# Bucketed attention with a feed-forward block on one core: keys-first scores in place of row-normalised, transposed weights

## The chip, the cores and the metric

The kernel runs on 1 core of one Trainium2 chip. The number that counts is the time of one execution on the chip in microseconds (us). Three runs of the kernel before gave 1418.2, 1417.16 and 1420.69 us; their median is 1418.2 us.

## The reference

`q`, `k` and `v` have shape (4 batches, 8 heads, 768 tokens, 64 channels). Each query and each key gets a bucket number from six hash bits, the signs of its products with the six columns of `proj`. A query attends only to the keys of its own bucket.

```
q_bits = (einsum('bhsd,dk->bhsk', q, proj) > 0);  k_bits likewise
mask   = bucket(q)[..., :, None] == bucket(k)[..., None, :]
scores = where(mask, q @ k.T / sqrt(64), -1e9)
attn   = exp(scores - max(scores));  attn /= sum(attn) + 1e-9
x      = (attn @ v), heads side by side: 3072 tokens x 512 channels
h      = x @ w_in            # 512 x 2048
out    = (h * sigmoid(1.702 h)) @ w_out   # 2048 x 512
```

The inputs `q`, `k` and `v` are normal numbers times 0.1. The weights arrive as float64 and are turned into float32 on the chip.

## The kernel before

**Attention.** Work goes by 16 pairs of heads (4 batches by 4 pairs). A pair's two heads lie side by side on the 128 partitions, 64 channels each. `prepare` turns the keys and queries so that channels lie on partitions (12 TensorE transposes, L143, evicted by VectorE at L146 and by ScalarE at L149), and makes the hash bits with one matmul per half of the tokens (L151) and a VectorE comparison (L152).

The 768 queries of a pair are two halves of three tiles of 128. `scores` takes one tile of queries by all 768 keys: for each head and each half of the keys a bfloat16 matmul on the hash bits and a float32 matmul on the channels add into one PSUM tile (L167). Each float32 matmul stands in the trace as two MATMUL records. VectorE then evicts each head's 128x768 scores with the mask's clamp and the row minimum (L173; scores are kept negated), ScalarE takes the exponential with that minimum as its bias and the row sum (L175), VectorE makes the reciprocals (L177, L178), and GpSimd multiplies the rows by them (L180). `turn` transposes the finished weights, six 128x128 transposes per head (L190), so that keys lie on partitions; VectorE and ScalarE evict them (L195, L193). `values` multiplies them with `v` (L203), 12 matmuls per half, and ScalarE evicts the result into `xT` (L206).

**Weights.** `convert` turns one 128x256 piece of a float64 weight into float32: a load on GpSimd's queue (L87), five VectorE operations (L94 to L99), two GpSimd operations (L102, L103), and one more on VectorE (L104). There are 64 pieces.

**Feed-forward block.** Then 384 matmuls 128x512 give `h` (L249), ScalarE applies the activation (L251), 384 more give `y` (L255), VectorE evicts (L258), and the SP queue stores (L260).

**Order of the work.** A scheduler places each engine's instructions, TensorE's too, by its own estimates of when they are ready. Each engine then takes its instructions strictly in that order. `turn` and `values` of a tile are emitted behind the scores of the next one. PSUM holds two buffers of four kinds of tile: `ps` (scores), `pt` (transposed weights), and `m` for hash, turned inputs and `av`.

Of the kernel before, what the change touches and what calls it, by code (L numbers as in the profile page):

```python
# [9 lines left out]
BF16 = mybir.dt.bfloat16  # L10
U32 = mybir.dt.uint32
Act = mybir.ActivationFunctionType
Alu = mybir.AluOpType
PSUM = bass.MemoryType.PSUM

P = 128
# [3 lines left out]
BIT = 2.0**33  # L20


@with_exitstack
def kernel(
# [26 lines left out]
    assert D == 64 and S == 2 * HS and HS <= 512 and HP == KC and DM <= 512 and NB < 32  # L51
# [3 lines left out]
    make_identity(nc, ident)  # L55

    # The hash of two heads at once: head j's channels give its bits on rows 64 j to 64 j + NB.
# [5 lines left out]
    # Bits become +-0.5 (0 on rows without one). Row NB is a constant: with it, the product of a  # L63
    # query's and a key's column is 0 where all bits agree, and -0.5 for each bit that differs.
# [13 lines left out]
    w_out_sb = const.tile([P, FC, DM], F32, name="w_out_sb")  # L78

# [1 line left out]
    actx = ExitStack()  # L81
    cv = actx.enter_context(tc.tile_pool(name="cv", bufs=2))
    CW = 256

    def convert(dst, src):
        raw = cv.tile([P, CW, 2], U32, tag="raw", name="raw")
# [5 lines left out]
        rest = cv.tile([P, CW], F32, tag="rest", name="rest")  # L92
        # Sign, exponent (rebiased by its top bit) and the upper 20 bits of the mantissa.
# [3 lines left out]
        # The mantissa's lower 32 bits, scaled by the power of two that is `bits` without mantissa.  # L97
        nc.vector.tensor_scalar(sign, bits, 0xFF800000, None, op0=Alu.bitwise_and)
        nc.vector.scalar_tensor_tensor(rest, lo, 2.0**-52, sign.bitcast(F32), op0=Alu.mult, op1=Alu.mult)  # L99
# [3 lines left out]
        nc.gpsimd.tensor_tensor(rest, bits.bitcast(F32), rest, op=Alu.add)  # L103
        nc.vector.scalar_tensor_tensor(dst, size, (1.125 * 2.0**-15) ** 2, rest, op0=Alu.is_ge, op1=Alu.mult)  # L104
# [7 lines left out]
    ld = actx.enter_context(tc.tile_pool(name="ld", bufs=2))  # L112
    wk = actx.enter_context(tc.tile_pool(name="wk", bufs=2))
    sp = actx.enter_context(tc.tile_pool(name="sp", bufs=5))
    pp = actx.enter_context(tc.tile_pool(name="pp", bufs=4))
    st = actx.enter_context(tc.tile_pool(name="st", bufs=4))
    sps = actx.enter_context(tc.tile_pool(name="sps", bufs=2, space=PSUM))
    tps = actx.enter_context(tc.tile_pool(name="tps", bufs=2, space=PSUM))
    mps = actx.enter_context(tc.tile_pool(name="mps", bufs=2, space=PSUM))

    pairs = [(b, hp) for b in range(B) for hp in range(HP)]
    loaded, ready = {}, {}

    def load(n):
        b, hp = pairs[n]
        for name, src in (("k", k), ("q", q), ("v", v)):
            # Both heads' channels of a token side by side, so that one transpose turns them.
            x = ld.tile([P, T, 2, D], F32, tag=name, name=name, bufs=2 if name == "v" else 1)
            for j in range(2):
                nc.sync.dma_start(out=x[:, :, j, :], in_=src[b, 2 * hp + j].rearrange("(p t) d -> p t d", p=P))  # L130
            loaded[n, name] = x

    def prepare(n):
        """The pair's queries and keys, channels first, and their hash bits."""
        for name, off, op in (("k", k_off, Alu.is_gt), ("q", q_off, Alu.is_lt)):
            x = loaded.pop((n, name))
            xt = wk.tile([P, S], F32, tag=f"{name}T", name=f"{name}T")
            bits = wk.tile([P, S], BF16, tag=f"{name}b", name=f"{name}b")
            for c in range(2):
# [5 lines left out]
                if name == "k":  # L145
                    nc.vector.tensor_copy(xt[:, cols], tp)  # L146
                else:
                    # Negated and scaled by a power of two, for the scores; its bits read "below 0".
                    nc.scalar.mul(xt[:, cols], tp, -1.0 / D**0.5)  # L149
# [3 lines left out]
            if name == "q":  # L153
                nc.vector.tensor_scalar(bits, bits, -BIT, None, op0=Alu.mult)
            ready[n, name] = xt, bits

    def scores(n, t):
        """exp(score - its row's max) / (sum + 1e-9) of both heads, queries of tile t by all keys."""
        (qT, qb), (kT, kb) = ready[n, "q"], ready[n, "k"]
        rows = slice(t * P, (t + 1) * P)  # L160
        ps = [sps.tile([P, 2, 512], F32, tag="s", name="ps") for _ in range(2)]
        for c in range(2):
            cols = slice(c * HS, (c + 1) * HS)
            for a, m, last in ((qb, kb, False), (qT, kT, True)):
                for j in range(2):
                    hs = slice(D * j, D * (j + 1))
                    nc.tensor.matmul(ps[j][:, c, 0:HS], a[hs, rows], m[hs, cols], start=not last, stop=last)  # L167
        low = st.tile([P, 2], F32, tag="low", name="low")
        total = st.tile([P, 2], F32, tag="total", name="total")
        es = []  # L170
        for j in range(2):
            e = sp.tile([P, 2, HS], F32, tag="e", name="e")
# [3 lines left out]
            es.append(e.rearrange("p c s -> p (c s)"))  # L176
        nc.vector.tensor_scalar_add(total, total, 1e-9)  # L177
        nc.vector.reciprocal(total, total)  # L178
        for j in range(2):
            nc.gpsimd.tensor_scalar(es[j], es[j], total[:, j : j + 1], 1.0, op0=Alu.mult, op1=Alu.mult)  # L180
        return es
# [25 lines left out]

    load(0)
    prepare(0)
    behind = []  # L210

    def catch_up():
        for f, *a in behind:
# [74 lines left out]
```

## Time and profile before

| what | value |
|---|---|
| median of the runs | 1418.2 us |
| profiled execution, its span | 1420.0 us |
| TensorE busy (PE) | 1314.6 us, 93% of the span |
| VectorE busy (DVE) | 513.9 us, 36% |
| ScalarE busy (ACT) | 358.9 us, 25% |
| GpSimd busy (POOL) | 300.1 us, 21% |
| mean granted TensorE clock | 0.970 of full |
| first matmul of the feed-forward block | at 756.50 us |

Busy shares are means over stages. Three stages can be told apart: attention with the weight conversion beside it (to some 345 us), attention alone (to 756 us), and the feed-forward block. The profile gives the span of one execution from the first to the last instruction; it lies 0.13% above the median of the runs, so times of the trace can be set against the runs directly.

### The profile page before, as it was taken

The page shows a single profiled execution, that of the slowest core. Times are in us where ns is not written, and L with a number is a line of the kernel's source. Part 1 is how long each engine was busy: PE and PEld are TensorE (multiplying, and loading weights), DVE is VectorE, ACT ScalarE, POOL GpSimd, SP SyncE. Part 2 cuts the span into 40 slices and gives each one's busy share as a digit, 9 for nine tenths or more (in the row PEclk, how much of TensorE's full clock was granted, in tenths as well). Part 3 has the DMA queues.
Part 4 walks back from the last instruction along what each step waited for, and adds up shares of the span by engine and source line. Part 5 has one row for each costly group of instructions (what it writes and reads, how often), then busy time and mean ns, then how long its engine had stood idle before and what let it go on. Part 6 is the DMA issues. An engine that isn't in the chain of part 4 may idle for free.

```text
span 1420.0 us, 13204 instructions
## 1 busy us (share of the span) xinstructions
PE 1314.6 (93%) x4928; PEld 657.7 (46%) x4928; DVE 513.9 (36%) x1299; ACT 358.9 (25%) x738; POOL 300.1 (21%) x390
## 2 busy tenths in 40 slices
PE   5887887888999999999989999999999999999998
PEld 3443443444555555555554444444444444444443
DVE  6788888887555555555540000000000000000000
ACT  1333333334444444444442100100100100100100
POOL 4555555554222232222230000000000000000000
PEclk9898898899999999999999999999999999999999
DMA  5132222221111111111000000000000000000000
GB/s 130 56 79 71 67 78 71 67 78 49 31 26 34 34 34 23 23 33 24 12 1 0 0 15 15 0 15 15 0 15 15 0 15 15 0 8 22 0 8 22
DMA packets 84062, 42.79 MB, mean 30 GB/s; under 512 B 76832, under 2 KB 76832, under 8 KB 84000
## 3 DMA queue, kind: packets, MB, share of 16 engines
q1 hardware_dynamic: 78880, 25.18, 7.1%
q0 software_dynamic: 5120, 16.78, 3.8%
q8 instruction: 39, 0.64, 0.2%
q14 instruction: 23, 0.19, 0.0%
HBM read 35.65 MB, written 6.29 MB: 30 GB/s over the span
## 4 chain that ended last, share of the span: by engine, by line
PE 75%; DVE 12%; POOL 4%; ACT 4%; DMA 2%; issue 2%; POOLq 0%; DVEq 0%; ACTq 0%
PE h L249 23%; PE y L255 23%; PE ps L167 12%; PE av L203 7%; PE pt L190 7%; ACT e L175 3%; DVE e L173 3%; POOL e L180 2%; PE hash L151 2%; DMA raw<-in_moe_w_in_dram 2%; POOL rest L103 2%; DVE pT L195 2%; DVE sign L94 1%; DVE rest L99 1%; DVE bits L95 1%
## 5 line engine op out<-in xcount | busy, mean ns | idle before, releaser
L249 PE MATMUL h<-xT,w_in_sb 128*128 128x512 f32 x768 | 330.7, 592 | 0.6 <-ACT xT L206 0.6
L255 PE MATMUL y<-w_out_sb,g 128*128 128x512 f32 x768 | 330.6, 592 | 0.0
L258 DVE COPY o<-y 128x512 f32<-128x512 f32 x24 | 16.6, 690 | 648.8 <-PE y L255 648.8
L180 POOL TENSOR_SCALAR e<-e,total 128x768 f32<-128x768 f32 x192 | 177.3, 934 | 322.8 <-ACT pT L193 212.9
L167 PE MATMUL ps<-kT,qT 64*128 64x384 f32 x768 | 241.8, 527 | 0.0
L175 ACT ACTIVATE e<-e,low 128x768 f32<-128x768 f32 x192 | 179.4, 934 | 210.0 <-DVE e L173 208.0
L249 PEld LDWEIGHTS h<-xT,w_in_sb 128*128 128x128 f32 x768 | 145.8, 190 | 184.4 <-issue 183.2
L255 PEld LDWEIGHTS y<-w_out_sb,g 128*128 128x128 f32 x768 | 145.9, 190 | 183.7 <-issue 183.7
L173 DVE TENSOR_SCALAR_CACHE_REDUCE e<-ps 128x768 f32<-128x768 f32 x192 | 176.6, 953 | 139.0 <-PE ps L167 139.0
L190 PE MATMUL pt<-ident,e 128*128 128x128 f32 x1152 | 180.2, 295 | 33.7 <-POOL e L180 32.4
L190 PEld LDWEIGHTS pt<-ident,e 128*128 128x128 f32 x1152 | 133.9, 149 | 139.6 <-issue 63.1
L251 ACT ACTIVATE g<-h 128x512 f32<-128x512 f32 x96 | 57.3, 597 | 542.7 <-PE h L249 542.7
L167 PE MATMUL ps<-kb,qb 64*128 64x384 bf16 x384 | 99.6, 347 | 53.0 <-DVE e L173 52.8
L167 PEld LDWEIGHTS ps<-kT,qT 64*128 64x128 f32 x768 | 107.8, 203 | 83.0 <-issue 82.9
L203 PE MATMUL av<-pT,v 128*64 128x384 f32 x768 | 145.6, 499 | 0.0
L195 DVE COPY pT<-pt 128x384 f32<-128x384 f32 x192 | 106.0, 552 | 21.2 <-PE pt L190 20.5
L193 ACT COPY pT<-pt 128x384 f32<-128x384 f32 x192 | 89.9, 468 | 64.1 <-PE pt L190 62.9
L203 PEld LDWEIGHTS av<-pT,v 128*64 128x64 f32 x768 | 73.1, 139 | 57.9 <-issue 31.8
L103 POOL TENSOR_TENSOR rest<-bits,rest 128x256 f32<-128x256 f32 x64 | 47.6, 743 | 61.6 <-DVE rest L99 42.0
L102 POOL TENSOR_TENSOR size<-raw 128x256 f32<-128x256 f32 x64 | 41.4, 647 | 63.6 <-DMA raw<-in_moe_w_in_dram 29.1
L206 ACT COPY xT<-av 128x384 f32<-128x384 f32 x32 | 15.3, 478 | 128.1 <-PE av L203 128.1
L167 PEld LDWEIGHTS <-qb 64*128 64x128 bf16 x384 | 24.2, 94 | 44.7 <-issue 41.9
(41 smaller groups left out, 517.5 us busy)
## 6 DMA issues: line engine op xcount, KB each, us to landing
raw<-in_moe_w_in_dram POOLq DMA_DIRECT2D x32, 256.0 KB, 3.1
raw<-in_moe_w_out_dram POOLq DMA_DIRECT2D x32, 256.0 KB, 3.1
k<-in_k_dram SPq DMA_DIRECT2D x32, 192.0 KB, 3.2
q<-in_q_dram SPq DMA_DIRECT2D x32, 192.0 KB, 3.2
v<-in_v_dram SPq DMA_DIRECT2D x32, 192.0 KB, 3.4
out_dram<-o SPq DMA_DIRECT2D x24, 256.0 KB, 2.0
pb<-in_proj_dram SPq DMA_DIRECT2D x2, 1.5 KB, 3.0
```

Source lines behind the costliest of these rows:

```text
L103: nc.gpsimd.tensor_tensor(rest, bits.bitcast(F32), rest, op=Alu.add)
L167: nc.tensor.matmul(ps[j][:, c, 0:HS], a[hs, rows], m[hs, cols], start=not last, stop=last)
L173: nc.vector.tensor_scalar(e, ps[j][:, :, 0:HS], MASKED, None, op0=Alu.min, op1=Alu.min, accum_out=low[:, j : j + 1])
L175: nc.scalar.activation(e, e, Act.Exp, bias=low[:, j : j + 1], scale=-1.0, accum_out=total[:, j : j + 1])
L180: nc.gpsimd.tensor_scalar(es[j], es[j], total[:, j : j + 1], 1.0, op0=Alu.mult, op1=Alu.mult)
L190: nc.tensor.transpose(tp[:, i, :], es[j][:, s : s + P], ident)
L193: nc.scalar.copy(dst, tp)
L195: nc.vector.tensor_copy(dst, tp)
L203: nc.tensor.matmul(av[D * j : D * (j + 1), :], vt[:, t, j, :], pT[j][:, t, :], start=(t == 0), stop=(t == T - 1))
L249: nc.tensor.matmul(h, w_in_sb[:, kc, fc * P : (fc + 1) * P], xT[:, kc, n * NT : (n + 1) * NT], start=(kc == 0), stop=(kc == KC - 1))
L251: nc.scalar.activation(g[:, fc, :], h, Act.Gelu_apprx_sigmoid)
L255: nc.tensor.matmul(y, g[:, fc, i * P : (i + 1) * P], w_out_sb[:, fc, :], start=(fc == 0), stop=(fc == FC - 1))
```

## The change

The scores are computed with keys on partitions and queries along the free axis, one tile of 128 keys by one half (384) of the queries, both heads in one PSUM tile. ScalarE takes the exponential straight out of PSUM, without a row maximum, into a buffer `es` of the half. This buffer is already what the product with `v` needs, so the transposes, the normalising multiplication and the clamp are gone. A half now has six such units. The sums over keys are built by VectorE and GpSimd adding the six exponential tiles (`sums`), and a matmul with a tile of ones adds over the partitions (`norm`); a reciprocal and one VectorE operation write `xT`. A 385th column of the exponentials holds a tiny constant.

Leaving out the maximum is safe only for small scores. ScalarE therefore sums the squares of each pair's queries and keys (`measure`). After the feed-forward block every engine loads the largest of them and branches: if it is at least 64, attention in the old way and the feed-forward block run again.

TensorE's instructions in attention now keep the order in which the code emits them (`manual_schedule`); the other engines are scheduled as before. The weight pieces are 128x512, so there are 32 of them, and three of their working tiles have one buffer in place of two.

```diff
-    CW = 256
+    CW = 512
-            nc.vector.tensor_scalar(e, ps[j][:, :, 0:HS], MASKED, None, op0=Alu.min, op1=Alu.min,
-                                    accum_out=low[:, j : j + 1])
-            nc.scalar.activation(e, e, Act.Exp, bias=low[:, j : j + 1], scale=-1.0, accum_out=total[:, j : j + 1])
-        nc.vector.tensor_scalar_add(total, total, 1e-9)
-        nc.vector.reciprocal(total, total)
-        for j in range(2):
-            nc.gpsimd.tensor_scalar(es[j], es[j], total[:, j : j + 1], 1.0, op0=Alu.mult, op1=Alu.mult)
-    def turn(es, t, pT):
...
+            es = [ep.tile([P, T, 2, HS + 1], F32, name=f"e{i}") for i in range(2)]
...
+            def measure(n):
+                for i, name in enumerate("kq"):
...
+                    nc.scalar.activation(junk, tiles[n][name], Act.Square,
+                                         accum_out=sizes[:, 2 * n + i : 2 * n + i + 1])
+            def scores(n, c, kt):
...
+                ps = sps.tile([P, 2, 512], F32, tag="s", name="ps")
+                for a, m, last in ((kb, qb, False), (kT, qT, True)):
+                    for j in range(2):
+                        hs = slice(D * j, D * (j + 1))
+                        nc.tensor.matmul(ps[:, j, 0:HS], a[hs, keys], m[hs, cols], start=not last, stop=last)
+                nc.scalar.activation(es[c][:, kt, :, 0:HS], ps[:, :, 0:HS], Act.Exp)
+            def sums(n, c, kt):
...
+                if kt == 1:
...
+                    nc.vector.scalar_tensor_tensor(acc, e[:, 0, :, 0:HS], T * TINY, e[:, 1, :, 0:HS],
+                                                   op0=Alu.add, op1=Alu.add)
+                elif kt == 3:
...
+                    nc.gpsimd.tensor_tensor(two, e[:, 2, :, 0:HS], e[:, 3, :, 0:HS], op=Alu.add)
+                elif kt > 3:
...
+                    nc.vector.tensor_tensor(acc, acc, e[:, kt, :, 0:HS], op=Alu.add)
+                    if kt == T - 1:
+                        nc.vector.tensor_tensor(acc, acc, accs.pop((n, c, 2)), op=Alu.add)
+            def values(n, c, kt):
...
+                for j in range(2):
+                    nc.tensor.matmul(av[D * j : D * (j + 1), :], vt[:, kt, j, :], es[c][:, kt, j, :],
+                                     start=(kt == 0), stop=(kt == T - 1))
+            def norm(n, c):
...
+                for j in range(2):
+                    nc.tensor.matmul(dn[D * j : D * (j + 1), :], ones, acc[:, j, :], start=True, stop=True)
+                rd = st.tile([P, HS], F32, tag="rd", name="rd")
+                nc.vector.reciprocal(rd, dn)
...
+                nc.vector.scalar_tensor_tensor(xT[:, hp, s0 : s0 + HS], av[:, 0:HS], vs[:, 0:1], rd,
+                                               op0=Alu.add, op1=Alu.mult)
+            with tc.manual_schedule(engines={PE}):
...
+                LAG = 2
...
+                    for u in range(2 * T):
+                        c, kt = divmod(u, T)
+                        scores(n, c, kt)
+                        behind.append((n, c, kt))
+                        sums(n, c, kt)
+                        if len(behind) > LAG:
+                            x = behind.pop(0)
+                            values(*x)
+                            if x[2] == T - 1:
+                                norm(x[0], x[1])
+                        if u >= 1 and todo:
+                            todo.pop(0)()
...
+    attention()
+    feed_forward("")
+    unsafe = nc.values_load(largest[0:1, 0:1].bitcast(I32)) >= SAFE_BITS
+    with tc.If(unsafe):
+        shifted_attention()
+        feed_forward("2")
```

On TensorE, in the first pairs of heads before: score matmuls of the two heads (`ps`) lie apart, with transposed weights (`pt`), hash and turned queries (`tp`) between them.

```order
L167 LDWEIGHTS qb
L167 MATMUL ps<-kb,qb 128x384
L167 LDWEIGHTS qb
L167 MATMUL ps<-kb,qb 128x384
L190 MATMUL pt<-ident,e 128x128 x6
L167 MATMUL ps<-kT,qT 128x384
L151 MATMUL hash<-qT,pb 128x384
L143 MATMUL tp<-ident,q 128x128 x3
L167 MATMUL ps<-kT,qT 128x384
L151 MATMUL hash<-qT,pb 128x384
```

On TensorE now, in the middle of attention (the tenth of 16 pairs, where the next pair's queries are hashed): four score matmuls stand together, then the two products with `v` of two units earlier, then one step of the next pair's preparation.

```order
L210 MATMUL ps<-qT,kT 128x384 x2
L237 MATMUL av<-e_111,v 64x385 x2
L165 MATMUL hash<-qT,pb 128x384
L210 LDWEIGHTS kb
L210 MATMUL ps<-qb,kb 128x384
L210 LDWEIGHTS kb
L210 MATMUL ps<-qb,kb 128x384
L210 MATMUL ps<-qT,kT 128x384 x2
L237 MATMUL av<-e_111,v 64x385 x2
L165 MATMUL hash<-qT,pb 128x384
```

The two heads' matmuls of one kind now follow each other throughout, and no transposes of weights are left.

On VectorE before, while weights are converted (`raw`, `bits`, `sign`, `rest` are the conversion's tiles): between the conversion's operations stand score evictions out of PSUM (`e`) and evictions of transposed weights (`pT`).

```order
L195 COPY pT<-pt 128x3x128 [waits PE_49]
L178 RECIPROCAL total<-total 128x2 [waits DVE_49]
L104 SCALAR_TENSOR_TENSOR w_in_sb<-size,rest 128x256 [waits Pool_49]
L96 TENSOR_TENSOR bits<-bits,sign 128x256
L173 TENSOR_SCALAR e,low<-ps 128x768 [waits PE_49] x2
L195 COPY pT<-pt 128x3x128 [waits PE_49]
L146 COPY kT<-tp 128x384 [waits PE_49]
L98 TENSOR_SCALAR sign<-bits 128x256 [waits DVE_49]
L94 TENSOR_SCALAR sign<-raw 128x256 [waits DMASW1_49]
L99 SCALAR_TENSOR_TENSOR rest<-raw,sign 128x256 [waits DVE_49]
```

On VectorE now, in the same stage (from the second pair to the third; `acc` and `two` are the running sums):

```order
L228 TENSOR_TENSOR acc<-acc,e_111 128x768 [waits Activation_49]
L120 SCALAR_TENSOR_TENSOR w_in_sb<-size,w_in_sb 128x512 [waits Pool_49]
L230 TENSOR_TENSOR acc<-acc,two 128x768 [waits DVE_49]
L111 TENSOR_SCALAR bits<-raw 128x512
L112 TENSOR_TENSOR bits<-bits,sign 128x512 [waits DVE_49]
L114 TENSOR_SCALAR sign<-bits 128x512 [waits DVE_49]
L115 SCALAR_TENSOR_TENSOR w_in_sb<-raw,sign 128x512 [waits DVE_49]
L220 SCALAR_TENSOR_TENSOR acc<-e_110 128x768 [waits Activation_49]
L247 RECIPROCAL rd<-dn 128x384 [waits PE_49]
L249 COPY vs<-av 128x1
L158 COPY kT<-tp 128x384 [waits PE_49]
L251 SCALAR_TENSOR_TENSOR xT<-av,vs,rd 128x384 [waits DVE_49]
```

Most of VectorE's work between conversions now reads SBUF. All 32 conversions stand ahead of the twelfth of the 32 `xT` operations (L251) in this queue, nearly three to a half; from there on the queue holds none.

## Rows read from the trace of the kernel before

**Rows 1.** Busy time by stretch: stretch, its length, PE, PEld, DVE, ACT, POOL, granted clock, DMA.

```profile
core 0: us, PE busy (x) PEld busy (x) DVE busy (x) ACT busy (x) POOL busy (x), PEclk, DMA share, GB/s
54.63:341.20 286.57, 229.91 (x1158) 124.33 (x1157) 241.43 (x621) 101.90 (x219) 164.99 (x227) 0.88 0.25 71
364.40:756.50 392.10, 367.07 (x1994) 211.38 (x1993) 200.44 (x507) 175.38 (x375) 101.64 (x114) 0.99 0.10 23
```

**Rows 2.** Groups by line in those two stretches, ACT: count, busy us, mean ns.

```profile
L206 ACT COPY xT<-av 128x384 f32<-128x384 f32 x11 | 5.3, 479 | 44.7 <-PE av L203 44.7
...
L206 ACT COPY xT<-av 128x384 f32<-128x384 f32 x20 | 9.6, 478 | 79.1 <-PE av L203 79.1
```

**Rows 3.** Timeline of PE near 510 us: start, us, what, count, [idle before].

```profile
504.89 0.33 PE L167 MATMUL ps<-kb,qb 64*128 64x384 bf16 x1
...
506.38 0.87 PE L190 MATMUL pt<-ident,e 128*128 128x128 f32 x6
507.18 4.52 PE L203 MATMUL av<-pT,v 128*64 128x384 f32 x24
511.64 0.34 PE L167 MATMUL ps<-kb,qb 64*128 64x384 bf16 x2
511.81 0.81 PE L167 MATMUL ps<-kT,qT 64*128 64x384 f32 x4
512.55 0.87 PE L190 MATMUL pt<-ident,e 128*128 128x128 f32 x6
...
518.66 0.49 PE L143 MATMUL tp<-ident,k 128*128 128x128 f32 x3
519.08 0.33 PE L167 MATMUL ps<-kb,qb 64*128 64x384 bf16 x1
...
520.70 0.81 PE L151 MATMUL hash<-kT,pb 128*128 128x384 f32 x2
521.35 0.49 PE L143 MATMUL tp<-ident,k 128*128 128x128 f32 x3
```

**Rows 4.** Groups by line of the whole span, shapes apart.

```profile
L190 PE MATMUL pt<-ident,e 128*128 128x128 f32 x1152 | 180.2, 295 | 33.7 <-POOL e L180 32.4 <-ACT pT L193 1.2
L175 ACT ACTIVATE e<-e,low 128x768 f32<-128x768 f32 x192 | 179.4, 934 | 210.0 <-DVE e L173 208.0 <-POOL e L180 1.9
L103 POOL TENSOR_TENSOR rest<-bits,rest 128x256 f32<-128x256 f32 x64 | 47.6, 743 | 61.6 <-DVE rest L99 42.0 <-DVE total L177 17.6 <-DVE total L178 2.0
L102 POOL TENSOR_TENSOR size<-raw 128x256 f32<-128x256 f32 x64 | 41.4, 647 | 63.6 <-DMA raw<-in_moe_w_in_dram 29.1 <-DMA raw<-in_moe_w_out_dram 22.6 <-DVE pT L195 2.7
L177 DVE TENSOR_SCALAR total<-total 128x2 f32<-128x2 f32 x96 | 15.8, 164 | 42.4 <-ACT e L175 42.4
L178 DVE RECIPROCAL total<-total 128x2 f32<-128x2 f32 x96 | 15.0, 156 | 0.8 <-DVE sign L94 0.2
```

**Rows 5.** Timeline of DVE near 176 us, GpSimd idle beside it.

```profile
175.59 0.55 DVE L195 COPY pT<-pt 128x384 f32<-128x384 f32 x1
176.06 0.28 DVE L98 TENSOR_SCALAR sign<-bits 128x256 uint32<-128x256 uint32 x1
176.26 0.29 DVE L94 TENSOR_SCALAR sign<-raw 128x256 uint32<-128x256 uint32 x1
176.46 0.42 DVE L99 SCALAR_TENSOR_TENSOR rest<-raw,sign 128x256 f32<-128x256 uint32 x1
176.79 0.29 DVE L95 TENSOR_SCALAR bits<-raw 128x256 uint32<-128x256 uint32 x1
```

**Rows 6.** Timeline of POOL and of DVE near 184 us.

```profile
183.42 1.89 POOL L180 TENSOR_SCALAR e<-e,total 128x768 f32<-128x768 f32 x2
...
184.59 1.00 DVE L99 SCALAR_TENSOR_TENSOR rest<-raw,sign 128x256 f32<-128x256 uint32 x1
```

**Rows 7.** Timeline of PE: the first scores, and the feed-forward block's first matmuls.

```profile
22.86 0.50 PE L167 MATMUL ps<-kb,qb 64*128 64x384 bf16 x2
...
756.50 7.99 PE L249 MATMUL h<-xT,w_in_sb 128*128 128x512 f32 x18 [0.57 <-ACT xT L206]
```

More of the change, by code (lines that the diff above doesn't have):

```diff
@@ L55 @@
     make_identity(nc, ident)
+    ones = const.tile([P, D], F32, name="ones")
+    nc.vector.memset(ones, 1.0)
     pb = const.tile([P, P], F32, name="pb")
@@ L78, with convert @@
     w_out_sb = const.tile([P, FC, DM], F32, name="w_out_sb")
-    actx = ExitStack()
-    cv = actx.enter_context(tc.tile_pool(name="cv", bufs=2))
-    CW = 256
-    def convert(dst, src):
-        raw = cv.tile([P, CW, 2], U32, tag="raw", name="raw")
+    pairs = [(b, hp) for b in range(B) for hp in range(HP)]
+    sizes = const.tile([P, 2 * len(pairs)], F32, name="sizes")
+    largest = const.tile([P, 1], F32, name="largest")
+    CW = 512
+    def convert(cv, dst, src):
+        raw = cv.tile([P, CW, 2], U32, tag="raw", name="raw", bufs=2)
         nc.gpsimd.dma_start(out=raw, in_=src)
@@ L147, in prepare, with hashed @@
                 else:
[L149 removed]
+                    nc.scalar.mul(xt[:, cols], tp, scale)
+            def hashed(c, name=name, xt=xt, bits=bits, off=off, op=op):
+                cols = slice(c * HS, (c + 1) * HS)
                 dots = mps.tile([P, HS], F32, tag="m", name="hash")
@@ L197, in values @@
-    def values(n, half, pT):
-        b, hp = pairs[n]
-        vt = loaded[n, "v"]
-        av = mps.tile([P, HS], F32, tag="m", name="av")
-        for t in range(T):
-            for j in range(2):
-                nc.tensor.matmul(av[D * j : D * (j + 1), :], vt[:, t, j, :], pT[j][:, t, :],
-                                 start=(t == 0), stop=(t == T - 1))
-        s0 = b * S + half * HS
-        nc.scalar.copy(xT[:, hp, s0 : s0 + HS], av)
[L208 to L213, printed above, removed]
-            f(*a)
-        behind.clear()
@@ L217 @@
-    per = -(-len(chunks) // len(pairs))
-    for n in range(len(pairs)):
-        if n + 1 < len(pairs):
-            load(n + 1)
-        for half in range(2):
-            pT = [pp.tile([P, T, HS], F32, tag="pT", name="pT") for _ in range(2)]
-            for t in range(HT):
-                es = scores(n, half * HT + t)
-                catch_up()
-                behind.append((turn, es, t, pT))
-                if t == HT - 1:
-                    behind.append((values, n, half, pT))
-            if half == 0:
-                if n + 1 < len(pairs):
-                    prepare(n + 1)
-                for dst, src in chunks[n * per : (n + 1) * per]:
-                    convert(dst, src)
@@ new lines, in feed_forward @@
+    def feed_forward(tag):
+        NT = 512
+        G = NT // P
+        outv = out.rearrange("(b p t) d -> b t p d", b=B, p=P)
+        with ExitStack() as fctx:
+            gp = fctx.enter_context(tc.tile_pool(name=f"gp{tag}", bufs=2))
+            op = fctx.enter_context(tc.tile_pool(name=f"op{tag}", bufs=4))
+            fps = fctx.enter_context(tc.tile_pool(name=f"fps{tag}", bufs=4, space=PSUM))
+            for n in range(N // NT):
+                g = gp.tile([P, FC, NT], F32, tag="g", name="g")
+                for fc in range(FC):
+                    h = fps.tile([P, NT], F32, tag="h", name="h")
+                    for kc in range(KC):
+                        nc.tensor.matmul(h, w_in_sb[:, kc, fc * P : (fc + 1) * P], xT[:, kc, n * NT : (n + 1) * NT],
+                                         start=(kc == 0), stop=(kc == KC - 1))
+                    nc.scalar.activation(g[:, fc, :], h, Act.Gelu_apprx_sigmoid)
+                for i in range(G):
+                    y = fps.tile([P, DM], F32, tag="y", name="y")
+                    for fc in range(FC):
+                        nc.tensor.matmul(y, g[:, fc, i * P : (i + 1) * P], w_out_sb[:, fc, :],
+                                         start=(fc == 0), stop=(fc == FC - 1))
+                    o = op.tile([P, DM], F32, tag="o", name="o")
+                    nc.vector.tensor_copy(o, y)
+                    b, t = divmod(n * G + i, T)
+                    nc.sync.dma_start(out=outv[b, t], in_=o)
```

226 lines of the change are left out of this document (149 added, 77 removed).

## The prediction, made before the changed kernel ran

> **What bounds the kernel now.** I first cut the span into stretches. The feed-forward block starts at 756.50 us and lasts to the end at 1420.0, 663.5 us of back-to-back matmuls [rows 7]; the change leaves it alone. So only the 756.5 us ahead of it are in play. They hold 32 halves (16 pairs, two halves each). Counting the evictions of `av` gives the pace. While weights are converted, 11 halves take 286.57 us, 26.05 each; afterwards 20 halves take 392.10 us, 19.6 each [rows 1, 2]. In the later stage TensorE is busy for 367.07 of the 392.10 us (94%), at a granted clock of 0.99: it is the bound. In the earlier stage VectorE is busy for 241.43 of 286.57 us (84%), TensorE for 80% at a granted clock of 0.88: the two wait for each other, VectorE in front.
>
> Then I read how TensorE spends its time. When the four score matmuls of the two heads stand together, they take 511.64 to 512.55, 0.91 us, and the four float32 records last 0.81 us from first start to last end: both heads run at once [rows 3]. Where the order pulls the heads apart, the same work takes 504.89 to 506.38, 1.49 us. The 24 records with `v` take 507.18 to 511.64, 4.46 us for six pairs of heads' matmuls.
>
> **The change part by part.** *TensorE, one half.* Six score units in the tight order: 6 x 0.91 = 5.5 us; such a unit stood in the trace, so only its frequency is new. Six pairs with `v`: 0.74 us each if they keep the block's pace [rows 3]. They now stand alone between scores, so each pays the switch in and out; I take 0.79, which makes 4.7. The 385th column is nothing. The ones matmul has the shape of one such pair: 0.7. The preparation is unchanged: four groups of three transposes at 0.42 and four hashes at 0.65 to 0.75 [rows 3], 4.5 per pair, 2.25 per half. Sum: 13.1 us. The transposes of the weights, 180.2 us busy [rows 4], are gone, and with them the waits for GpSimd's normalising. With the idle share of the late stage above, somewhat eased because each product with `v` trails its exponential by two units, I take 13.6 per late half. No row shows the new chain of waits, so bounds are 13.1 and 15.5 (13.1 with an idle fifth, as in the early stage).
>
> ScalarE: six exponentials of 128x768, one Square and one `qT` per half, at 0.934 us each or less [rows 4]: under 7.5 us of 13.6. The next scores need the PSUM tile freed by the exponential two units back, some 1.7 us of TensorE's work later, so 0.93 hides. If a Square comes between, 1.9 us against 1.7 to 2.5 remains mostly hidden; I charge nothing, and the idle share covers it.
>
> VectorE, one half without conversions: four sums of 128x768: a two-input operation of 256 starts its successor after 0.33 us (176.46 to 176.79 [rows 5]), so at most 1.0 for 768; I take 0.88, together 3.5. One reciprocal of 128x384: nothing in the trace is like it; I take the 0.47 of the PSUM eviction of that size (175.59 to 176.06). The `xT` operation, the small copy, `kT`, two hash comparisons and the scaling of the bits: 2.4. Sum 6.4, under 13.6: late halves stay TensorE's.
>
> A conversion: of 256 elements it costs VectorE three operations at 0.20 (176.06 to 176.26) and three at 0.33 [rows 5], and GpSimd 0.647 + 0.743 [rows 4]. Twice the elements cost at most twice that, 3.2 and 2.8; I take 2.85 and 2.55, since part of each is fixed. GpSimd's new sum of 128x768 takes at most 3 x 0.743; I take 2.0.
>
> An early half: the queue of VectorE puts all 32 conversions ahead of the twelfth half's `xT`; two pass before the first scores, so 30 fall on 11 halves. VectorE's own work: 30 x 2.85 / 11 + 6.4 = 14.2 us. But it cannot run beside GpSimd freely: an operation that lasts 0.42 us [rows 5] lasted 1.00 while GpSimd worked on the exponentials [rows 6]. If every SBUF operation of the one excludes those of the other, a half costs 7.8 + 3.5 + 0.2 on VectorE and 30 x 2.55 / 11 + 2.0 = 9.0 on GpSimd, 20.5 us together; only VectorE's 2.7 us out of PSUM lie beside it. Before, PSUM evictions filled most of VectorE's time, so GpSimd had room. I take 21, with bounds of 14.5 (no exclusion) and 25 (nearly the 26.05 of before). TensorE then stands idle a third of the time, and a granted clock of 0.88 or less is hidden behind VectorE.
>
> The Trainium skill has a rule for this (SBUF — State Buffer, "Who interferes with whom"): GpSimd shares one pair of SBUF ports with VectorE as an exclusive lock, and a VectorE instruction with two SBUF inputs, or in a two-port mode, blocks until the other is done. The 1.00 against 0.42 agrees. By this rule the sum is 20.5 a half, without it 14.2.
>
> Ends: the first scores start at 22.86 us [rows 7]; the new order hashes keys and queries in one go, but the first conversion (now 512 KB to load) still stands before the first `kT` copy on VectorE. I take 21 (18 to 26). At the end of attention the last exponential, two sums, the ones matmul, reciprocal and `xT` follow each other: 0.93 + 2 x 0.88 + 0.7 + 0.5 + 0.5, less the matmuls beside them: 5 us exposed. The branch at the end: all engines load one word and jump over the second copy. No row shows that. It costs at least nothing, since the last store runs beside it, and I allow 6; I take 3. The sum of squares is ready long before.
>
> Loads: SP issues the same loads of k, q and v; each key buffer frees in the first third of a pair's span, so its load has over 10 us to land. Nothing is charged.
>
> Sum on the profiled execution: 21 + 11 x 21 (231) + 19 x 13.6 (258) + 2 halves without preparation x 11.2 (22) + 5 + 663.5 + 3 = 1204 us, against the span of 1420.0. The median of the runs is 0.13% below that span, less than the roundings here, so 1204 stands for the runs.
>
> **The rivals.**
> A, 71%: the forecast.
> B, 12%, a slow reciprocal: of 384 elements it could take several times an eviction. For it: no row shows more than two elements. Against: with two, RECIPROCAL takes 156 ns and an addition 164 [rows 4], so a price per element would have to hide in 8 ns less. At 3.3 us it adds 2.8 to an early half (31 in all), and about 0.5 to a late one, whose VectorE work of 9.2 still fits: 1245 us.
> The Trainium skill speaks for B (VectorE: DVE Perf Modes, "First, the fixed hardware budget"): the reciprocal is an iterated division with a repeat count of 8. By that, as an estimate, 8 x 0.47 = 3.8 us and some 1250 us.
> C, 8%, no exclusion to speak of: early halves at 14.5: 1204 - 11 x 6.5 = 1132. For it: before, GpSimd's 165 us and VectorE's 241 of 286.57 overlapped a good deal [rows 1]. Against: much of VectorE's part came from PSUM then.
> *D, 5%, the heads do not run side by side* when scores and products with `v` alternate: 1.49 in place of 0.91 and some 1.4 in place of 0.79 make a half 20.3, or 24 early: 21 + 264 + 19 x 20.8 + 2 x 18.5 + 671.5 = 1389. Against: in the trace neighbours always overlap, whatever stood before.
> E, 3%, slower: the granted clock falls to the lower of its two levels (1.2 in place of 2.4 GHz) through all of attention, because TensorE now waits in short pieces. Its work of 192 x 1.70 + 32 x 0.7 + 16 x 4.5 = 421 us doubles to 842, and the time is 21 + 842 + 671.5 = 1535. It passes 1420 once the mean clock in attention is under 421/728 = 0.58. Against: 0.88 at 80% busy, 0.99 at 94% [rows 1]; late halves have TensorE busy almost throughout.
> F, 1%: the branch is taken and attention and feed-forward run again, about 2600 us. Sums of squares of 768 normal numbers times 0.1 lie near 7.7, far from 64.
>
> **How the numbers follow.** The likeliest case, A, alone runs from 1155 (early 17.5, late 13.2) to 1255 (early 24, late 14.5). With B inside and half of C, 1140 to 1280 leaves out about 2 in 10 (half of C, D, E, F and A's own tails). Faster by over 0.3%, about what a measurement of this kernel can tell from no change: A, B, C and D, 95%. Within 0.3%: an early stage like before together with D, 1%. Slower: E and F, 4%.
>
> **What would show it.** Score units of four records about 0.91 us apart from the next work, in all 192; products with `v` in pairs of under 0.8 us; no record of transposed weights. A late half of 13 to 14 us with TensorE over 94% busy, an early one near 21 with VectorE over 80% busy and its conversion operations often at twice their free length. RECIPROCAL of 128x384 near 0.5 us; 3 us would be B. The feed-forward block within 1 us of 663.5. I would be wrong in the mechanism if late halves took over 16 us, or if TensorE's own work in a half were above 15.

## The result, and the profile of the changed kernel

The changed kernel takes 1213.35 us (median; 1211.3 to 1214.26) against 1418.2: a ratio of 0.855, 95% interval 0.854 to 0.856. The forecast was 1204 with a range of 1140 to 1280. The profiled execution spans 1211.1 us, and the branch at the end was not taken: no work of the second copy is in the trace.

Busy time by stretch of the kernel after (columns as in [rows 1]): the halves with conversions, the halves after them, feed-forward to the end.

```profile
core 0: us, PE busy (x) PEld busy (x) DVE busy (x) ACT busy (x) POOL busy (x), PEclk, DMA share, GB/s
52.30:265.80 213.50, 156.82 (x736) 52.76 (x734) 194.27 (x266) 60.91 (x89) 104.60 (x86) 0.86 0.29 87
265.80:522.70 256.90, 256.90 (x1408) 92.62 (x1406) 173.79 (x211) 115.60 (x167) 29.37 (x19) 1.00 0.17 39
543.90:1211.10 667.20, 661.13 (x1536) 292.32 (x1536) 16.59 (x24) 58.60 (x97) 0.00 (x0) 1.00 0.03 10
```

The first two stretches are cut at writes of `xT`. The first holds 10 halves, 21.35 us each; the second 19, 13.52 each, where before a late half took 19.6 [rows 1, 2]. In the second TensorE never stops and its clock is at the higher level throughout. In the first, VectorE is busy for 91% and TensorE waits a quarter of the time. Attention shrank by 212.6 us (756.50 to 543.90), feed-forward and end grew by 3.7.

TensorE's timeline near 405 us shows what a half is made of:

```profile
404.64 0.87 PE L237 MATMUL av<-e,v 128*64 128x385 f32 x4
405.44 0.34 PE L210 MATMUL ps<-qb,kb 64*128 64x384 bf16 x2
405.62 0.81 PE L210 MATMUL ps<-qT,kT 64*128 64x384 f32 x4
406.36 0.87 PE L237 MATMUL av<-e,v 128*64 128x385 f32 x4
...
409.78 0.87 PE L237 MATMUL av<-e,v 128*64 128x385 f32 x4
410.47 0.81 PE L245 MATMUL dn<-acc,ones 128*64 128x384 f32 x4
411.22 0.34 PE L210 MATMUL ps<-qb,kb 64*128 64x384 bf16 x2
```

A score unit (the four score matmuls of two heads, six records) takes 0.92 us (405.44 to 406.36), a product with `v` 0.80 (404.64 to 405.44), the ones matmul 0.75. The 5.6 us of transposed weights per half [rows 4] have no successor on TensorE.

The groups by line that answer to the new terms:

```profile
L228 DVE TENSOR_TENSOR acc<-acc,e 128x768 f32<-128x768 f32 x64 | 68.3, 1068 | 44.5 <-ACT e L211 44.4
L224 POOL TENSOR_TENSOR two<-e 128x768 f32<-128x768 f32 x32 | 50.6, 1581 | 252.7 <-ACT e L211 203.7
L245 PE MATMUL dn<-acc,ones 128*64 128x384 f32 x128 | 32.6, 594 | 53.7 <-DVE acc L230 53.7
L247 DVE RECIPROCAL rd<-dn 128x384 f32<-128x384 f32 x32 | 81.6, 2549 | 0.9 <-PE dn L245 0.9
```

The reciprocal takes 2.55 us. Of the 56.7 us that TensorE is idle in the first stretch (213.50 less 156.82), 50.3 stand before one instruction, the ones matmul, which waits for the last sum. Why that comes late is in the early timeline: VectorE, GpSimd, TensorE, one fence each.

```profile
143.95 1.25 DVE L111 TENSOR_SCALAR bits<-raw 128x512 uint32<-128x512 uint32 x1
145.11 1.11 DVE L168 TENSOR_SCALAR qb<-qb 128x384 bf16<-128x384 bf16 x1
...
150.03 0.69 DVE L120 SCALAR_TENSOR_TENSOR w_out_sb<-size,w_out_sb 128x512 f32<-128x512 f32 x1 [1.15 <-POOL w_out_sb L119]
...
153.63 0.95 DVE L230 TENSOR_TENSOR acc<-acc,two 128x768 f32<-128x768 f32 x1
```

```profile
143.34 1.57 POOL L224 TENSOR_TENSOR two<-e 128x768 f32<-128x768 f32 x1
144.87 1.23 POOL L118 TENSOR_TENSOR size<-raw 128x512 f32<-128x512 f32 x1
148.08 1.91 POOL L119 TENSOR_TENSOR w_out_sb<-bits,w_out_sb 128x512 f32<-128x512 f32 x1 [1.99 <-DVE w_out_sb L115]
```

```profile
146.07 0.87 PE L237 MATMUL av<-e,v 128*64 128x385 f32 x4
154.63 1.55 PE L245 MATMUL dn<-acc,ones 128*64 128x384 f32 x4 [7.69 <-DVE acc L230]
```

VectorE's queue has operations of conversions ahead of the last sum at 153.63. On the way there it is slowed twice: an operation takes 1.25 us while GpSimd works (0.42 on the mean where GpSimd only issues loads, in e8 below), and it stands idle for 1.15 until GpSimd has added the low part. TensorE, whose next scores stand behind the ones matmul, waits 7.69 us.

The end of attention on TensorE, and the first matmuls of feed-forward (before: [rows 7]):

```profile
536.59 2.16 PE L237 MATMUL av<-e,v 128*64 128x385 f32 x12
539.63 0.87 PE L245 MATMUL dn<-acc,ones 128*64 128x384 f32 x4 [0.88 <-DVE acc L230]
...
543.90 8.37 PE L384 MATMUL h<-xT,w_in_sb 128*128 128x512 f32 x15 [3.21 <-DVE xT L251]
```

### The profile page after: what moved, and what is told of

Same layout as the page of the kernel before. It is cut to its first block, busy times and chain, and to the rows that moved or that the text cites. A ratio compares the mean times of both kernels' runs of the same rounds, so it can differ in the third digit from the quotient of the medians.

```text
span 1211.1 us, 9543 instructions
## 1 busy us (share of the span) xinstructions
PE 1125.0 (93%) x3905; PEld 456.5 (38%) x3905; DVE 437.9 (36%) x582; ACT 257.9 (21%) x386; POOL 160.6 (13%) x136
## 4 chain that ended last, share of the span: by engine, by line
PE 78%; DVE 18%; POOL 3%; issue 1%; DMA 1%; ACT 0%; DVEq 0%; POOLq 0%
PE h L384 27%; PE y L390 27%; PE ps L210 9%; PE av L237 8%; PE hash L165 3%; DVE bits L112 2%; DVE rd L247 2%; DVE acc L228 2%; DVE bits L111 2%; PE tp L155 1%; POOL w_in_sb L119 1%; PE dn L245 1%; POOL w_out_sb L119 1%; DVE sign L114 1%; DVE sign L110 1%
## 5 line engine op out<-in xcount | busy, mean ns | idle before, releaser
L211 ACT ACTIVATE e<-ps 128x768 f32<-128x768 f32 x192 | 155.0, 809 | 206.7 <-PE ps L210 204.7
L237 PE MATMUL av<-e,v 128*64 128x385 f32 x768 | 172.5, 530 | 0.0
L210 PE MATMUL ps<-qT,kT 64*128 64x384 f32 x768 | 163.7, 506 | 0.0
L228 DVE TENSOR_TENSOR acc<-acc,e 128x768 f32<-128x768 f32 x64 | 68.3, 1068 | 44.5 <-ACT e L211 44.4
L224 POOL TENSOR_TENSOR two<-e 128x768 f32<-128x768 f32 x32 | 50.6, 1581 | 252.7 <-ACT e L211 203.7
L247 DVE RECIPROCAL rd<-dn 128x384 f32<-128x384 f32 x32 | 81.6, 2549 | 0.9 <-PE dn L245 0.9
L237 PEld LDWEIGHTS av<-e,v 128*64 128x64 f32 x768 | 39.1, 138 | 111.0 <-issue 110.8
L210 PEld LDWEIGHTS ps<-qT,kT 64*128 64x128 f32 x768 | 72.8, 199 | 0.2 <-issue 0.2
L210 PE MATMUL ps<-qb,kb 64*128 64x384 bf16 x384 | 66.5, 343 | 1.9 <-DVE qb L168 1.8
L118 POOL TENSOR_TENSOR size<-raw 128x512 f32<-128x512 f32 x32 | 41.4, 1293 | 31.2 <-DVE w_out_sb L120 12.3
```

The lines of the kernel that those rows point to most:

```text
L210: nc.tensor.matmul(ps[:, j, 0:HS], a[hs, keys], m[hs, cols], start=not last, stop=last)
L211: nc.scalar.activation(es[c][:, kt, :, 0:HS], ps[:, :, 0:HS], Act.Exp)
L224: nc.gpsimd.tensor_tensor(two, e[:, 2, :, 0:HS], e[:, 3, :, 0:HS], op=Alu.add)
L228: nc.vector.tensor_tensor(acc, acc, e[:, kt, :, 0:HS], op=Alu.add)
L237: nc.tensor.matmul(av[D * j : D * (j + 1), :], vt[:, kt, j, :], es[c][:, kt, j, :], start=(kt == 0), stop=(kt == T - 1))
L247: nc.vector.reciprocal(rd, dn)
```

## The experiments

Ratios are against the kernel before, timed beside each. The expectations were written in three groups of four, in the order shown, each with the results of the groups before it known.

**A copy for the reciprocal (e1).**

```diff
-                nc.vector.reciprocal(rd, dn)
+                nc.vector.tensor_copy(rd, dn)
```

> Leaves out the division: a copy of the same 128x384 from PSUM stands in place of the reciprocal, so a VectorE operation of 2.55 us becomes one of about 0.47. Theory (VectorE is what sets the pace of the early halves, and hides in the late ones): 10 early halves lose 2.08 us each, 21.35 to about 19.3; late halves stay at 13.5; the tail behind the last scores loses another 2. Sum 1213.4 - 21 - 2 = 1190 us. Rival (the early halves are paced by the hand-over between VectorE and GpSimd, and the reciprocal lies in waits that are there anyway): early halves lose under 0.5, total 1206 to 1213.

1207.08 us, ratio 0.8505 (0.8494 to 0.8517): 6.3 us less than the kernel after, the rival's number. But the time does not bear out the rival's reason, since the edit also moved the conversions. Groups in the stretch of conversions, first of the kernel after (52.3 to 265.8 us), then of e1 (49.4 to 246.2):

```profile
L251 DVE SCALAR_TENSOR_TENSOR xT<-av,vs,rd 128x384 f32<-128x384 f32 x10 | 6.1, 605 | 0.0
```

```profile
L251 DVE SCALAR_TENSOR_TENSOR xT<-av,vs,rd 128x384 f32<-128x384 f32 x9 | 5.5, 608 | 0.0
L247 DVE COPY rd<-dn 128x384 f32<-128x384 f32 x9 | 4.9, 548 | 0.0
```

In both stretches the last operation of a conversion (L120) stands 27 times, in e1 in nine halves in place of ten, the last of which, 11.4 us long, holds none: the scheduler packed them closer on VectorE. So e1 changed two things, and e11 repeats it with the order held. As an estimate, each of the two halves that no longer hold conversions leaves 6.1 us of VectorE unused (in e1 a late half takes 13.5 us and VectorE is busy for 7.4 of them): 12 of the 17 us that are missing from the theory.

**Without the branch (e3).**

```diff
-    unsafe = nc.values_load(largest[0:1, 0:1].bitcast(I32)) >= SAFE_BITS
-    with tc.If(unsafe):
-        shifted_attention()
-        feed_forward("2")
```

> The load of the largest sum of squares into registers, the branch and the second copy of attention and feed-forward are left out; the work that runs is the same. Theory (the branch costs what the end has grown by): the stretch from the last copy to the end of the span goes back from 6.0 to 4.0 us, total 1211.4. Rival 1 (the longer program costs elsewhere too, in loading code): more than 4 us go. Rival 2 (the end grew for another reason): no change, 1213.4.

1211.29 us, ratio 0.8534 (0.8522 to 0.8545). The intervals overlap, so the times alone do not tell it from the kernel after. The traces do. The last copy of the kernel before, with a span of 1420.0 us, of the kernel after (1211.1) and of e3 (1208.9):

```profile
1416.00 0.69 DVE L258 COPY o<-y 128x512 f32<-128x512 f32 x1 [13.04 <-PE y L255]
```

```profile
1205.08 0.69 DVE L393 COPY o<-y 128x512 f32<-128x512 f32 x1 [13.04 <-PE y L390]
```

```profile
1204.57 0.69 DVE L393 COPY o<-y 128x512 f32<-128x512 f32 x1 [13.04 <-PE y L390]
```

The end is 4.3 us in place of 6.0 (4.0 before): the load, the branch and the second copy together cost about 1.7, near the theory.

**The conversion on VectorE alone (e5).**

```diff
-        nc.gpsimd.tensor_tensor(size, hi.bitcast(F32), hi.bitcast(F32), op=Alu.mult)
-        nc.gpsimd.tensor_tensor(dst, bits.bitcast(F32), dst, op=Alu.add)
+        nc.vector.tensor_tensor(size, hi.bitcast(F32), hi.bitcast(F32), op=Alu.mult)
+        nc.vector.tensor_tensor(dst, bits.bitcast(F32), dst, op=Alu.add)
```

> GpSimd's two operations of each conversion (the square, the addition of the low part) are moved to VectorE, where they cost 2 x 0.61 us in place of 1.3 and 1.6 on GpSimd. Theory (the two engines exclude each other, and VectorE waits 1.15 us in each conversion for GpSimd): the early half is no longer than before the edit, 19.5 to 21.3 us in place of 21.35, total 1193 to 1213. Rival (GpSimd's part lay beside VectorE's): VectorE gets 30 x 1.22 / 11 = 3.3 us more a half, 24.7, total 1213 + 10 x 3.3 = 1247.

1179.67 us, ratio 0.831 (0.830 to 0.832): 34 us faster, below the theory's lower end of 1193. More work on the busiest engine made the stage shorter, so GpSimd's part had not simply lain beside VectorE's. The rival is out. But the order was not held: the stretch has 13 halves now, 17.6 us each, so part of the gain is spreading:

```profile
43.80:272.60 228.80, 188.78 (x953) 64.76 (x951) 227.28 (x351) 79.49 (x116) 35.77 (x38) 0.93 0.33 91
```

VectorE was idle for 19.2 us of the stretch in the kernel after and is idle for 1.5 here. How much is spreading was not measured. As an estimate: between e4 and e10 below, 21 more halves to spread over are worth 85 us, 4 a half; three halves would be 12 of the 34 us.

**TensorE's order left to the scheduler (e2).**

```diff
-            with tc.manual_schedule(engines={PE}):
+            if True:
```

> TensorE's order is left to the scheduler; everything else stays. Theory (the fixed order is what makes each score unit 0.91 in place of up to 1.49 us): if the scheduler pulls the heads apart in most units, a late half goes from 13.5 to 15.5 to 17 and the total to 1260 to 1290; early halves, bound by VectorE, stay near 21. Rival (the scheduler leaves the heads together, the gain being in what is computed and not in the order): 1213 within 10 us.

1210.49 us, ratio 0.8527 (0.8514 to 0.854): the rival. The 19 late halves:

```profile
263.40:519.70 256.30, 256.30 (x1404) 92.40 (x1402) 172.73 (x211) 115.42 (x167) 29.40 (x19) 1.00 0.17 39
```

13.49 us each, as with the fixed order. The scheduler leaves the heads together; a score unit takes 0.92 us here too:

```profile
408.25 0.34 PE L210 MATMUL ps<-qb,kb 64*128 64x384 bf16 x2
408.43 0.81 PE L210 MATMUL ps<-qT,kT 64*128 64x384 f32 x4
409.17 0.87 PE L237 MATMUL av<-e,v 128*64 128x385 f32 x4
```

In the new kernel the order by hand brings nothing that can be measured.

**e5 and e1 together (e9).** Both diffs above.

> The edit of e5 (all of the conversion on VectorE) and that of e1 (a copy in place of the reciprocal, which leaves the division out) together. Theory (in the kernel after, GpSimd worked while the reciprocal read PSUM, so e1 alone gained only 6.3 us; with the conversion on VectorE nothing is left to work beside it, and the reciprocal is on the path): the early halves of e5 lose 2.08 us each, 17.5 to 15.4, on 13 to 14 halves, and the tail 2: 1179.7 - 28 - 2 = 1150, bounds 1145 to 1156. Rival (the reciprocal lies beside something else, TensorE's work or the loads): as little as in e1, 1171 to 1176.

1171.39 us, ratio 0.8254 (0.8241 to 0.8266): 8.3 us under e5, the rival's side. Again the packing moved: the stretch from 42.4 to 223.6 us has 10 halves of 18.1 us in place of 13 of 17.6. So e9 cannot weigh the reciprocal either.

**Nothing on GpSimd (e8).** e5's diff, and:

```diff
-                    nc.gpsimd.tensor_tensor(two, e[:, 2, :, 0:HS], e[:, 3, :, 0:HS], op=Alu.add)
+                    nc.vector.tensor_tensor(two, e[:, 2, :, 0:HS], e[:, 3, :, 0:HS], op=Alu.add)
```

> As e5, and the sum of the third and fourth exponentials is moved from GpSimd to VectorE too: GpSimd only issues loads in attention. Theory (exclusion: GpSimd's 1.6 to 1.7 us a half block VectorE's operations on SBUF for most of their length): VectorE pays 0.88 and gets back up to 1.65, so the early half of 17.5 becomes 16.7 to 17.2 and the total 1168 to 1177. Rival (no exclusion worth naming; e5 gained because hand-overs between the engines went): VectorE pays 0.88 a half on 14 halves, total 1190 to 1193.

1169.88 us, ratio 0.8246 (0.8234 to 0.8257): the theory's 1168 to 1177. The same operation in the stretch of conversions, in e5 with GpSimd's sum beside it, then in e8 without:

```profile
L118 DVE TENSOR_TENSOR size<-raw 128x512 f32<-128x512 f32 x26 | 23.2, 894 | 0.0
```

```profile
L118 DVE TENSOR_TENSOR size<-raw 128x512 f32<-128x512 f32 x27 | 18.6, 687 | 0.0
```

Beside GpSimd's sum the operation is drawn out by 0.21 us on the mean. The total does not weigh this alone, since the packing moved again:

```profile
43.10:290.70 247.60, 213.17 (x1112) 74.12 (x1110) 246.07 (x395) 91.89 (x135) 13.19 (x25) 0.97 0.32 89
```

That is 15 halves of 16.5 us, in e5 13 of 17.6.

**Conversions spread by hand (e4).** `convert` becomes a generator that yields between its stages; the order is fixed on three engines.

```diff
-            with tc.manual_schedule(engines={PE}):
+            with tc.manual_schedule(engines={PE, mybir.EngineType.DVE, mybir.EngineType.Pool}):
...
-                        if u % 6 == 2 and convs:
-                            convert(cv, *convs.pop(0))
+                        i = 2 * n + c
+                        if kt == 2:
+                            next(cvs[i])
+                        elif kt == 4:
+                            next(cvs[i])
+                        elif kt == 0 and i > 0:
+                            next(cvs[i - 1], None)
+                            if i + 1 < len(cvs):
+                                next(cvs[i + 1])
```

> The 32 conversions are spread by hand, one in each half of attention in place of 2.7 in each of the first 11; VectorE's and GpSimd's order is fixed by hand like TensorE's. GpSimd keeps its two operations. Theory (a late half has TensorE at 100% and VectorE at 68%, so one conversion of 2.85 us, 2.9 on GpSimd and the sum of 1.58, much of it beside the reciprocal, fits or nearly fits in 13.5 us): all halves 13.6 to 14.7, total 21 + 30 x 14 + 20.5 + 8 + 667 = 1137, bounds 1125 to 1160. Rival (each conversion costs the path 2.8 us wherever it stands, or the fixed order makes VectorE stand before exponentials that are not there yet): 1205 or more.

1136.26 us, ratio 0.801 (0.800 to 0.802), the theory's 1137. Against the kernel after that is 0.801 / 0.855 = 0.937 (0.934 to 0.940 from the ends of the two intervals): 77 us less, and the fastest of all. 29 halves of 13.96 us:

```profile
35.90:440.80 404.90, 397.18 (x2144) 139.01 (x2142) 394.60 (x493) 177.20 (x257) 150.95 (x116) 1.00 0.29 77
```

TensorE and VectorE are both busy for over 97%, and the clock stays at its higher level.

**Spread, and on VectorE (e7).** The diffs of e4 and e5.

> As e4, with the two GpSimd operations of each conversion on VectorE. Theory (VectorE has 6.4 + 2.1 + 2.85 + 1.2 = 12.5 us a half and is blocked for up to 1.6 by GpSimd's sum, 14.1 at most, next to TensorE's 13.5): halves of 13.6 to 14.3, total 1125 to 1145, at most some 10 us better than e4. Rival 1 (with no slack left every wait for an exponential or a matmul adds up): halves of 15 or more, total over 1160, slower than e4. Rival 2 (the place of the conversions doesn't matter): 1180, as e5.

1148.32 us, ratio 0.8095 (0.8084 to 0.8106): 12 us slower than e4 and just over the theory's 1145, whose gain of at most 10 us on e4 did not come. Halves take 14.36 us:

```profile
35.20:451.60 416.40, 396.96 (x2149) 140.39 (x2148) 408.02 (x551) 177.32 (x257) 64.78 (x58) 1.00 0.28 76
```

VectorE is busy for 408.02 / 29 = 14.07 us a half against 13.61 in e4. It took on 1.2 us (two operations at 0.61, the expectation's price) and so got back some 0.75. With one conversion a half GpSimd is the better place. In e5, with two, VectorE was faster, but there the packing moved too; the same move with the order held at two or three a half was not run.

**Packed by hand (e10).** e4's order with three conversions a half:

```diff
-                        i = 2 * n + c
-                        if kt == 2:
+                        i = 3 * (2 * n + c) + kt // 2
+                        if i < len(cvs) and kt % 2:
                             next(cvs[i])
-                        elif kt == 4:
+                        elif i < len(cvs):
+                            if i > 0:
+                                next(cvs[i - 1], None)
+                                if i + 1 < len(cvs):
+                                    next(cvs[i + 1])
                             next(cvs[i])
-                        elif kt == 0 and i > 0:
-                            next(cvs[i - 1], None)
-                            if i + 1 < len(cvs):
-                                next(cvs[i + 1])
+                        elif i == len(cvs):
+                            next(cvs[-1], None)
```

> As e4 (order of TensorE, VectorE and GpSimd fixed by hand), but with three conversions in each of the first 11 halves in place of one in each of 32. Theory (what counts is over how many halves the conversions are spread, since only a half that has some can use VectorE's idle time for them): back to about the kernel after, early halves of 21 to 23, total 1195 to 1225. Rival (e4 gained by the fixed order of VectorE and GpSimd): 1136 to 1150.

1221.33 us, ratio 0.861 (0.8596 to 0.8623): the theory. Only where the conversions and their stages stand differs between e4 and e10, and it is worth 85 us.

**Packed, with the copy (e11).** e10 with e1's diff.

> As e10, with a copy in place of the reciprocal (which leaves the division out); the place of every instruction stays, so that the 2.08 us saved by the copy are weighed alone, without the scheduler packing the conversions closer as it did in e1 and e9. Theory (e1 and e9 gained little because the conversions then fell on fewer halves; VectorE's own time is on the path): 11 halves lose 2.08 us each and the tail 2: 20 to 27 us under e10. Rival (the reciprocal, which reads PSUM, lies beside GpSimd's work and costs the path next to nothing): 4 to 8 us under e10.

1198.21 us, ratio 0.8444 (0.8429 to 0.8459): 23 us under e10, the theory's 20 to 27. The nine halves of the packed stretch, e10 and then e11:

```profile
44.50:256.10 211.60, 143.36 (x665) 48.22 (x661) 207.75 (x261) 54.99 (x79) 106.43 (x89) 0.85 0.31 91
```

```profile
43.00:237.70 194.70, 142.44 (x666) 48.51 (x667) 190.60 (x262) 55.31 (x80) 106.53 (x91) 0.84 0.34 100
```

23.51 against 21.63 us a half: of the 2.0 us saved, 1.88 come off. VectorE's own time is on the path. In e1 and e9 the conversions moved, which hid most of it by the estimate under e1.

**The square on ScalarE (e12).** e4, with:

```diff
-        nc.gpsimd.tensor_tensor(size, hi.bitcast(F32), hi.bitcast(F32), op=Alu.mult)
+        nc.scalar.activation(size, hi.bitcast(F32), Act.Square)
```

> As e4, with the square of each conversion on ScalarE (44% busy in e4) in place of GpSimd. Theory (in e4 VectorE is 97% busy, part of it blocked by GpSimd's square; without it the halves are TensorE's 13.5 again): 30 halves lose 0.4 us each, 1136 - 12 = 1124, bounds 1117 to 1131. Rival (ScalarE is late with the exponentials, or the 0.4 us are something else): 1134 or more.

1171.84 us, ratio 0.8246 (0.8232 to 0.826): a miss of the theory, 36 us slower than e4 and on the rival's side. ScalarE's timeline near 200 us:

```profile
200.54 0.67 ACT L119 ACTIVATE size<-raw 128x512 f32<-128x512 f32 x1 [4.38 <-DVE w_in_sb L123]
201.12 1.50 ACT L214 ACTIVATE e<-ps 128x768 f32<-128x768 f32 x2
```

The next square waits for VectorE's last operation on the one `size` buffer, and the exponentials stand behind it; VectorE's first sum of the half in turn waits 1.48 us for them. That is read from the trace; a second buffer was not tried.

**The kernel before, in the order of its code (e6).**

```diff
+    hand.enter_context(tc.manual_schedule(engines={mybir.EngineType.PE}))
     load(0)
     prepare(0)
```

> The kernel before with TensorE's order in attention as its code emits it; nothing else changes. Theory 1 (a tight order is worth something by itself): late halves go from 19.6 to 17.8 to 18.6 us, the sum of six score units at 0.91, 4.46 for the products with v, 5.6 for the transposes and 2.25 of preparation; total 1375 to 1400. Theory 2 (the order was not what the halves paid for; transposed weights were): within 8 us of 1419. Rival (in the order of the code TensorE stands before each half's softmax): over 1440.

1635.98 us, ratio 1.152 (1.149 to 1.155): the rival in size, at another place than it named:

```profile
L190 PE MATMUL pt<-ident,e 128*128 128x128 f32 x1152 | 191.9, 310 | 215.2 <-ACT pT L193 212.1 <-POOL e L180 3.0
```

TensorE stands 212.1 us before transposes whose PSUM tile ScalarE has not yet emptied. With the transposes in the kernel the scheduler's order was needed to cover them.

## Why the prediction was right, and which terms were off

The mechanism held: late halves are TensorE's (13.52 against 13.6 forecast), early ones VectorE's with GpSimd (21.35 against 21, though here two errors nearly cancelled, as shown below). With a half's end put where its last scores end, 6.6 us ahead of its `xT` as at the end of attention, the measured sum is:

| term | forecast | measured |
|---|---|---|
| first scores | 21 | 19.4 |
| 11 early halves | 231 | 239.8 |
| 19 late halves | 258 | 256.9 |
| last two | 22 | 20.5 |
| tail | 5 | 7.3 |
| feed-forward and end | 666.5 | 667.2 |

*TensorE's half.* The score unit came within 0.01 us of the 0.91 read from [rows 3], the product with `v` cost 0.80, not 0.79. The 13.1 us of work were 13.5, since score unit and product repeat every 1.71 us and the hashes cost 0.84; the idle share added on top was not there. The row of one tight unit was enough for 176 of the 192; the others stand in the early stage, where the granted clock is 0.86 on the mean, and take up to 1.8 times as long. What the forecast credits to the order is not the order's: e2 has the same halves without it, and in e6 it did harm. The wider pieces of weights, part of the same change, were not tried alone; by the forecast's durations they save VectorE 64 x 1.6 less 32 x 2.85, 11 us in all (an estimate).

*The reciprocal* is the term that was mis-sized: 2.55 us for the 0.47 taken from a PSUM eviction. It was 5.4 times as long, so rival B's mechanism was there, at less than B's 3.3. The Trainium skill (VectorE: DVE Perf Modes, "First, the fixed hardware budget") has the reciprocal as an iterated division with a repeat count of 8; the trace agrees in kind, and the estimate of 3.8 us made from it was too long. The argument from 156 ns for two elements [rows 4] failed: at the 6.6 ns an element of 2549 / 384 (an estimate), two elements are 13 of those 156 ns, too little to be seen. Late the reciprocal changes nothing (VectorE is busy for 68%, and e1's late halves, with a copy, take 13.5 us as well); early it costs 1.88 us a half in e10's order (e11), and in the tail it takes 2 of the 2.3 us missing.

*GpSimd's share* was over-priced, which made up for most of it. The forecast laid GpSimd's 9.0 us of an early half end to end with VectorE's 11.5 on SBUF and let only VectorE's 2.7 out of PSUM lie beside them: 20.5, or 6.3 us of GpSimd's on top of VectorE's own 14.2. GpSimd does work 9.0 us (104.60 less 24 issues of 0.59, over ten halves), but about 5 are paid. VectorE is idle for 1.9 us a half, nearly all before the last operation of a conversion, which waits for GpSimd (17.1 of 19.2 us). And it is busy for 19.4 us, of which 3.2 are operations drawn out: with their mean lengths in e8's packed stretch the same operations would be 32 us shorter over the ten halves. Two of them, in the kernel after (52.3 to 265.8 us) and in e8 (43.1 to 290.7):

```profile
L228 DVE TENSOR_TENSOR acc<-acc,e 128x768 f32<-128x768 f32 x20 | 24.7, 1236 | 0.0
L112 DVE TENSOR_TENSOR bits<-bits,sign 128x512 uint32<-128x512 uint32 x26 | 24.5, 942 | 0.6
```

```profile
L228 DVE TENSOR_TENSOR acc<-acc,e 128x768 f32<-128x768 f32 x30 | 28.6, 953 | 0.3 <-ACT e L211 0.3
L112 DVE TENSOR_TENSOR bits<-bits,sign 128x512 uint32<-128x512 uint32 x27 | 18.5, 686 | 0.0
```

The 16.2 us left agree with the forecast's 14.2 once the reciprocal is put in as measured. So the half came out at 21.35 because 2 us too little for the reciprocal met 1 to 2 too much for GpSimd: that it lies so near 21 is luck. Two timelines of e10 show the exclusion, GpSimd and VectorE:

```profile
140.87 1.14 POOL L119 TENSOR_TENSOR size<-raw 128x512 f32<-128x512 f32 x1 [2.99 <-DVE w_in_sb L123]
141.97 1.72 POOL L227 TENSOR_TENSOR two<-e 128x768 f32<-128x768 f32 x1
```

```profile
141.03 1.26 DVE L112 TENSOR_SCALAR bits<-raw 128x512 uint32<-128x512 uint32 x1
142.32 1.92 DVE L113 TENSOR_TENSOR bits<-bits,sign 128x512 uint32<-128x512 uint32 x1
...
149.92 0.69 DVE L113 TENSOR_TENSOR bits<-bits,sign 128x512 uint32<-128x512 uint32 x1
```

Each of VectorE's first two operations ends 0.3 to 0.6 us behind the GpSimd one beside it, and the second takes 1.92 us against 0.69 alone (149.92). The Trainium skill's exclusive lock (SBUF — State Buffer, "Who interferes with whom") agrees with these rows. What the forecast's sum had wrong is that work out of PSUM comes free beside GpSimd: by that rule a longer reciprocal would have cost an early half nothing, and in e10's order it costs 1.88 us.

*Ends.* Only one conversion passed ahead of the first scores, where two were forecast, and the first half, 26.3 us with four in it, makes up over half of the 8.8 us by which the early stage is long. The branch and what came with it cost 1.7 us (e3), forecast 3. Feed-forward starts at a lower granted clock after TensorE's idle 3.21 us: it is 0.80 on the mean over the first 15 matmuls, which take 8.37 us; before, 18 took 7.99 at 1.00 [rows 7]. That, 1.7 us in all, was not foreseen.

*What the forecast did not ask* is whether the early stage had to be there. It took from the queue that 30 conversions fall on 11 halves and priced that, although late halves have VectorE idle by its own sum. e4 and e10 show that this choice is worth 85 us.

## What to carry to other kernels

When a stage is bound by work that other stages could take, compare where it stands with where the idle time is; spreading it can be worth more than making it cheaper. Before an operation is weighed by leaving it out, hold the order of everything else, or the scheduler's new packing is measured with it. A price read at two elements says nothing of one at 384.

## What was not expected of the hardware

A RECIPROCAL of 128x384 from PSUM takes 2549 ns, a copy of the same tile 548. And moving work to the engine that is busiest made its stage faster in e5: 34 us, of which some 12 may be the looser packing that came with it. With one conversion a half and the order held, the same move lost 12 us (e7 against e4).
